# Attention and a mixture of experts on one core: rows of an intermediate at a pitch of 2112 bytes, V loaded for two pairs, a view of the output for each write, and the order made anew

## The chip, the cores and the metric

The kernel runs on one core of a Trainium2 chip. The metric is the device time of one execution in microseconds (us), median over several runs. TensorE (PE), VectorE (DVE), ScalarE (ACT) and GpSimd (POOL) compute. SyncE (SP) issues the plain transfers of this kernel, POOL the indirect ones, which gather or scatter rows by index.

## What is computed

```python
scores = 0.125 * q @ k.T              # 4 batches, 8 heads, 768 positions, width 64
scores = where(col < 4 or 0 <= row - col < 128, scores, -1e9)
x = softmax(scores) @ v               # written as 3072 tokens x 512, heads side by side
e = argmax(x @ w_gate)                # one of 8 experts for each token
g = softmax(x @ w_gate)[e] * sigmoid((x @ w_output_gate)[e])
out[token] = g * (relu(x[token] @ w1[e]) @ w2[e])    # w1: 512 x 1024, w2: 1024 x 512
```

## The kernel before

**Attention** goes over 16 pairs of heads, four to a batch (`pair`). For a pair, SP loads q, k and V (384 KB each, V as pieces of 512 bytes), POOL scales q in place (L1097), PE makes the scores of six tiles of 128 rows (L1113), DVE masks them and takes the maximum (L1122, L1125), ACT the exponential (L1129). PE turns the result (L1149), ACT copies it to `f` (L1152), POOL makes the masked halves `g` and `f` (L311), and PE multiplies by V (L1200) into `oA` and `oB`. The first four columns go a way of their own: `pk` on POOL (L1169), a turn on PE (L1175), a copy to `hlk`, three small transfers to `psk` and a matmul (L1212). The logits of the gate are summed up by POOL in `lg` (L1246). The pair's 768 x 128 block of x is stored by SP into the DRAM tensor `xd` (L1272).

**`xd`** has one row for each token and a row of zeros ahead: 512 values of x and one value `den`, the token's weight g. In float32 a row is 2052 bytes, so that nearly all rows, and the 512-byte pieces that a pair writes into them, begin off any multiple of 64 bytes.

**Routing** of a batch (`gate_route`) is small work on DVE, POOL and PE: which expert, and which place in the expert's list. After the second and the third batch two slots each for the fullest experts are set up, four early slots of 256 tokens. After the last batch the rest is dealt to 13 slots of 64 to 384 tokens by `final_table`, some 250 small DVE instructions (L484, L690 to L777) that give indices `idx` and experts `exp_i`.

**A slot** gathers its tokens' rows from `xd` to `xg` (POOL, L802), turns them on PE (L862), splits them into a coarse part `xh` (ACT) and a rest `xl` (DVE, L867), multiplies by the expert's first weights (L981, three products for each tile), applies relu with the same split (`hh` on ACT L893, `hl` on DVE L896), multiplies by the second weights (L1019), scales by `den`, which ACT copies to `sc` (L885), and scatters `y` to the output (POOL, L878). Weights come as 512 KB pieces to `raw` and are split by ACT (L837) and DVE (L841). The names `wa`, `wb`, `wc` with `h` or `l` are buffers of split weights.

**Order.** The work is recorded first (`Plan.op`), with an assumed duration, what it reads and writes, and a wished time `at`, made of the pair's or slot's number and of offsets in the table `AT`. `Plan.order` then deals the operations to the engines in turn, among those that could start nearly at once the one with the lowest `at`. The order is fixed when the program is built. Each engine runs its instructions in that order, and a waiting instruction holds up all that stand behind it on its engine or queue. The assumed durations, among them `size` and `busy` of transfers, do nothing but set this order.

**Waits for writes.** Two writes to one tensor are ordered by a wait. All 28 scatters name the whole of `out`, so each waits until the one before has landed.

Of the kernel before, what the change touches and what calls it, by code (L numbers as in the profile page):

```python
# [7 lines left out]
F32 = mybir.dt.float32  # L8
# [19 lines left out]
XW = DM + 1  # L28
SCALE = 0.125
# [19 lines left out]
SOFT = 1810  # L49
SLOT0, STEP, PLAIN, FSTEP = 182180, 20000, 1, 800  # L50
# [4 lines left out]
    "load": -19780, "v": 10768, "vs": 163198, "sinkv": -13952, "scale0": 28418, "scale1": -104693, "scale2": 64567,  # L55
    "s0": 4872, "s1": 1285, "s2": 725, "s3": 1220, "s4": 5238, "s5": 1946, "fold": -23950, "exp": 61170, "tr0": 39353,
    "tr1": 74543, "tr2": 36830, "trc": 21273, "mask": -30694, "pack": 5280, "guard": -60086, "skT": -9303, "hl": -24231,
# [202 lines left out]
def act(n, k=1):  # L260
    return {"took": 165 + 0.83 * n, "busy": 60 + 0.83 * n}
# [21 lines left out]
def moe_kernel(tc, qT, kx, vx, vs, wgo, w1, w2, nsink, window, out):  # L283
# [7 lines left out]
    with ctx:  # L291
# [9 lines left out]
        xd = dram.tile([NTOK + 1, XW], F32, name="xd")  # L301
# [98 lines left out]
        def small_loads():  # L400
            q = nc.sync

            def load():
                q.dma_start(out=wgt, in_=wgo)
                for j, src in enumerate((nsink, window)):
                    q.dma_start(out=nsw_i[:, j, :], in_=src.bitcast(I32).partition_broadcast(P))
                q.dma_start(out=xd[0, 0:DM].rearrange("(p c) -> p c", p=P), in_=tab[:, 0, 0, 0:4])
                q.dma_start(out=xd[0:1, DM:XW], in_=tab[0:1, 0, 0, 0:1])
            pl.op("SP", 2500, load, w=["wgt", "nsw_i", "xd0"], size=64, busy=2400, at=3000)
            pl.op("DVE", 1500, scalars, r=["nsw_i"], at=30000)  # L410
# [8 lines left out]
        req, rdd, rpos = (st([P, T, E], F32, n) for n in ("eq", "dd", "pos"))  # L419
        rohb = st([P, T, E], BF16, "ohb")  # L420
# [6 lines left out]
        def gate_route(p, b, lg, at, step, counted=None):  # L427
# [72 lines left out]
            def d2():  # L500
                nc.vector.scalar_tensor_tensor(out=rden, in0=rz, scalar=1.0, in1=rden, op0=ALU.add, op1=ALU.mult)
                nc.vector.reciprocal(out=rden, in_=rden)
# [38 lines left out]
            v(dve(12, 2), d2, r=["z", "den"], w=["den"])  # L541
# [327 lines left out]

        def put(p, key, ysk, m, sck, where, rows_, ids, idk, at):  # L870
# [9 lines left out]
            p.op("ACT", fn=scale_, r=[ysk, sck], w=[yk], at=at, **act(m))  # L880
            p.op("POOL", 1200, write, r=[yk, idk], w=[("out", key)], at=at, size=512 * P * 4, busy=1200, land=1000)

# [19 lines left out]
        def slot(p, k, size, ids, idk, xds, n, at, plain=False, reg=None, part=None, behind=()):  # L902
# [17 lines left out]
            if half:  # L920
# [24 lines left out]
                put(p, (k, 0), ys, m, scs[0], out.rearrange("n (a c) -> (n a) c", a=2), 2 * NTOK, lambda: ids(2, 0), idk, at + 5000)  # L945
# [65 lines left out]
            for tiles in ((2,), (0, 1)) if nt == 3 else (range(nt),):  # L1011
# [11 lines left out]
                for s in tiles:  # L1023
                    put(p, (k, s), ys[s], DM, scs[s], out, NTOK, lambda s=s: ids(1, s), idk, at + 12000)
# [27 lines left out]
        for fam, n, pool in (("q", 3, "qk"), ("k", 3, "qk"), ("e", 2, "qk"), ("v", 2, "bp"), ("vsr", 1, "bp"), ("x", 2, "bp"),  # L1052
# [3 lines left out]
                             ("hh", 4, "m0"), ("y", 2, "m0")):  # L1056
# [10 lines left out]
        def pair(p):  # L1067
# [125 lines left out]
            def av(kt):  # L1193
                def fn():
                    v_, f_, g_ = get(v), get(f), get(g)
                    for t, src in ((kt, f_), (kt + 1, g_)):
                        for a in range(2) if t < T else ():
                            r = slice(a * D, (a + 1) * D)
                            o = get(oA)[r, t, :] if t < 4 else get(oB)[r, t - 4, :]
                            nc.tensor.matmul(out=o, lhsT=v_[:, kt, r], rhs=src[:, kt, a, :], start=t == kt == 0 or t == kt + 1 == 4,  # L1200
# [54 lines left out]
            def norm(g):  # L1255
# [8 lines left out]
                def fn():  # L1264
# [8 lines left out]
                  w=[("xd", b, hp)], at=(at, "st"), size=P * 4 * S, busy=400)  # L1273
# [210 lines left out]
        with mctx:  # L1484
# [58 lines left out]
```

## Time and profile before

| | |
|---|---|
| three runs | 583.05, 587.39 (median), 591.72 us |
| the profiled execution | 590.12 us, its span 588.2 us |
| PE, DVE, ACT, POOL busy | 519.1, 346.5, 280.7, 193.9 us |
| mean granted clock of PE | 0.955 of full speed |
| DMA | 112.60 MB, 191 GB/s over the span |

The span is the time from the first to the last instruction, 1.9 us less than the execution's own time. A busy time is the union of an engine's instructions. The clock is granted by a throttle in two levels, 1.0 (2.4 GHz) and 0.5 (1.2 GHz).

### The profile page before, as it was taken

What the parts mean: (1) busy time and instruction counts of PE and PEld (TensorE: products, weight loads), DVE (VectorE), ACT (ScalarE), POOL (GpSimd) and SP (SyncE); (2) the same over time, 40 slices, a digit from 0 to 9 for tenths busy, and PEclk for the clock granted to TensorE, in tenths of its full rate; (3) what the DMA queues carried; (4) which work ended last, traced back from release to release, by engine and by line L of the source; (5) the groups of instructions that cost most, each with busy time, mean ns of one, the idle gap of its engine ahead of it and who ended that gap; (6) DMA issues with size and microseconds to landing.
All of it is one profiled execution on the core that took longest, in us unless ns stands there. A gap on an engine that the chain in (4) does not pass through costs nothing. (4 is left out here: it accounts for less than half of the span.)

```text
span 588.2 us, 10368 instructions
## 1 busy us (share of the span) xinstructions
PE 519.1 (88%) x3480; PEld 402.6 (68%) x3480; DVE 346.5 (59%) x802; ACT 280.7 (48%) x741; POOL 193.9 (33%) x296
## 2 busy tenths in 40 slices
PE   4998799987889899995889899999999878999992
PEld 2565576654556585784769598898778766787971
DVE  5765777768668837489985235425636445465420
ACT  3665667754655645434434325525435445256320
POOL 8546676566475611035011131212210302101010
PEclk9998889978979999996999899999999989999998
DMA  7474757648996149825448954627797728967640
GB/s 222 145 121 118 142 117 191 118 114 204 323 317 102 42 145 174 290 63 184 168 129 294 344 200 149 213 108 244 263 329 267 233 76 306 336 217 264 203 163 18
DMA packets 68959, 112.60 MB, mean 191 GB/s; under 512 B 8316, under 2 KB 35200, under 8 KB 68898
## 3 DMA queue, kind: packets, MB, share of 16 engines
q1 hardware_dynamic: 64434, 97.94, 56.4%
q0 software_dynamic: 4464, 13.91, 6.7%
q8 instruction: 30, 0.49, 0.3%
q14 instruction: 31, 0.25, 0.2%
HBM read 98.26 MB, written 13.25 MB: 190 GB/s over the span
## 5 line engine op out<-in xcount | busy, mean ns | idle before, releaser
L1129 ACT ACTIVATE e<-s,nmx 128x132 f32<-128x132 f32 x192 | 69.8, 371 | 49.1 <-DVE nmx L1125 44.2
L1113 PE MATMUL s<-k,q 64*128 64x260 f32 (+1 forms) x384 | 69.6, 442 | 12.9 <-POOL q L1097 6.2
L878 POOL DMA_INDIRECT out_dram<-y,idx x20 | 22.2, 1110 | 147.1 <-ACT y L875 96.6
L896 DVE SCALAR_TENSOR_TENSOR hl<-s,hh 128x512 fp32r<-128x512 f32 (+1 forms) x36 | 26.7, 747 | 58.4 <-ACT hh L893 58.3
L1113 PEld LDWEIGHTS s<-k,q 64*128 64x128 f32 x384 | 37.4, 205 | 29.5 <-ACT e L1129 14.3
L893 ACT ACTIVATE hh<-s 128x512 fp32r<-128x512 f32 (+1 forms) x36 | 23.0, 645 | 72.3 <-PE s L981 69.2
L802 POOL DMA_INDIRECT xg<-xd,idx x21 | 23.5, 1119 | 93.4 <-PE tp L862 65.8
L1122 DVE COPY_PREDICATED s<-maskf,s 128x256 f32<-128x256 int32 x80 | 33.9, 424 | 28.0 <-PE s L1113 24.0
L1097 POOL TENSOR_SCALAR q<-q 128x256 f32<-128x256 f32 x48 | 41.5, 875 | 22.2 <-DMA q<-in_qT_dram 16.0
L1125 DVE TENSOR_REDUCE nmx<-s 128x2 f32<-128x264 f32 x96 | 41.5, 432 | 3.3
L1129 ACT ACTIVATION_READ_ACCUMULATOR e<-s,nmx 128x1 f32 x192 | 38.7, 201 | 0.0
L311 POOL TENSOR_SCALAR_AFFINE_SELECT g<-f 128x512 f32<-128x512 f32 (+1 forms) x48 | 27.1, 565 | 23.5 <-ACT f L1152 23.3
L1149 PE MATMUL tp<-ident,e 128*128 128x128 f32 x192 | 33.0, 301 | 1.8 <-DVE lw L1236 1.0
L1152 ACT COPY f<-tp 128x512 f32<-128x512 f32 x48 | 28.1, 588 | 13.1 <-PE tp L1149 12.6
L875 ACT ACTIVATE y<-oA,sc 128x512 f32<-128x512 f32 (+1 forms) x18 | 11.7, 651 | 41.0 <-PE oA L1019 34.6
L867 DVE TENSOR_TENSOR xl<-tp,xh 128x512 fp32r<-128x512 f32 x23 | 15.5, 686 | 26.2 <-ACT xh L865 26.2
L1149 PEld LDWEIGHTS tp<-ident,e 128*128 128x128 f32 x192 | 23.5, 153 | 10.0 <-issue 3.7
L311 POOL TENSOR_SCALAR_AFFINE_SELECT f<-f 128x512 f32<-128x512 f32 (+1 forms) x48 | 26.9, 561 | 3.3
L1200 PE MATMUL oA<-f,v 128*64 128x128 f32 x256 | 27.1, 291 | 0.0
L878 POOL DMA_INDIRECT out_dram<-y,idx_e x8 | 9.7, 1214 | 49.1 <-ACT y L875 24.5
L1265 DVE TENSOR_TENSOR x<-tp,rs 128x512 f32<-128x512 f32 (+1 forms) x32 | 17.5, 550 | 13.8 <-PE tp L1262 13.7
L862 PE MATMUL tp<-ident,xg 128*128 128x128 f32 (+1 forms) x112 | 16.0, 271 | 4.2 <-ACT hr L935 2.5
(549 smaller groups left out, 1540.2 us busy)
## 6 DMA issues: line engine op xcount, KB each, us to landing
raw<-in_w_dram SPq DMA_DIRECT2D x96, 512.0 KB
v<-in_vx_dram SPq DMA_DIRECT2D x16, 384.0 KB
xd<-x SPq DMA_DIRECT2D x16, 384.0 KB
k<-in_kx_dram SPq DMA_DIRECT2D x15, 396.0 KB
q<-in_qT_dram SPq DMA_DIRECT2D x15, 384.0 KB
wa2h<-in_w_dram SPq DMA_DIRECT2D x4, 512.0 KB
wa2l<-in_w_dram SPq DMA_DIRECT2D x4, 512.0 KB
wa1h<-in_w_dram SPq DMA_DIRECT2D x3, 512.0 KB
```

The source lines that it names most:

```text
L311: nc.gpsimd.affine_select(out=ap, in_=ap if src is None else src, pattern=pattern, compare_op=op, fill=fill, base=base, channel_multiplier=cm)
L802: nc.gpsimd.indirect_dma_start(out=p.get(key), out_offset=None, in_=xd[0:n + 1, :], in_offset=bass.IndirectOffsetOnAxis(ap=ids(), axis=0))
L878: nc.gpsimd.indirect_dma_start(out=where, out_offset=bass.IndirectOffsetOnAxis(ap=ids(), axis=0), in_=p.get(yk)[:, 0:m], in_offset=None, b ...
L896: nc.vector.scalar_tensor_tensor(out=p.get(hl)[:, :, 0:n], in0=p.get(ps)[:, :, 0:n], scalar=0.0, in1=p.get(hh)[:, :, 0:n].bitcast(F32), op ...
L1097: nc.gpsimd.tensor_scalar(out=c, in0=c, scalar1=SCALE, scalar2=None, op0=ALU.mult)
L1113: nc.tensor.matmul(out=get(s)[:, a, o0:P + CW], lhsT=get(q)[r, t * P:(t + 1) * P], rhs=get(k)[r, k0:k0 + P + CW - o0], start=True, stop=True)
L1122: nc.vector.copy_predicated(out=both[:, :, 4:CW], mask=bc(maski[:, 1, 4:CW], 1, 2), data=z[:, :, 0:P])
L1125: nc.vector.tensor_reduce(out=get(nmx)[:, t, :], in_=both, axis=AX.X, op=ALU.max, negate=True)
L1129: nc.scalar.activation(out=get(e)[:, t, a, :], in_=get(s)[:, a, P:P + CW], func=AF.Exp, bias=get(nmx)[:, t, a:a + 1], scale=1.0, accum_out ...
L1149: nc.tensor.transpose(out=get(tp)[:, i, :], in_=get(e)[:, 2 * j + i // 2, i % 2, 4:CW], identity=ident)
L1152: nc.scalar.copy(out=get(f)[:, two].rearrange("p t a r -> p (t a) r"), in_=get(tp))
L1200: nc.tensor.matmul(out=o, lhsT=v_[:, kt, r], rhs=src[:, kt, a, :], start=t == kt == 0 or t == kt + 1 == 4, stop=False, skip_group_check=True)
```

## The change

- A row of `xd` has 528 values (`XP`), 2112 bytes, a multiple of 64. `den` is written 16 times into the row's end, so the small store goes from 4 to 64 bytes for each token, and the reciprocal before it from 6 to 96 columns. A gather brings 2112 bytes for each token.
- V is loaded for two pairs by one transfer of 768 KB, in pieces of 1024 bytes, 8 transfers in place of 16, into tiles of twice the size.
- Each scatter names a view of `out` of its own, declared disjoint from the others, and does not wait for the one before.
- All four buffers of `y` lie in the pool that opens when attention is done; before, two were there from the start.
- In the planner, a store of x counts as 786 KB in place of 393 KB, V as 904 KB, the store of `den` as 400 KB in place of 3 bytes. ACT's assumed durations are changed a little. The table `AT`, `SOFT` and `SLOT0` have new numbers, and the order comes out new on all engines.

```diff
+XP = 528
-SOFT = 1810
-SLOT0, STEP, PLAIN, FSTEP = 182180, 20000, 1, 800
+SOFT = 7200
+SLOT0, STEP, PLAIN, FSTEP = 153718, 20000, 1, 800
...
-    "n0": -84793, "n1": 56715, "xm": -63859, "st": -71391, "rt": 46575, "ft": 3923, "near": 77,
+    "add": -71892, "n0": -64048, "n1": 74649, "xm": -90144, "st": -74470, "rt": 75760, "ft": 46913, "near": 73,
...
-        xd = dram.tile([NTOK + 1, XW], F32, name="xd")
+        xd = dram.tile([NTOK + 1, XP], F32, name="xd")
...
-                nc.vector.reciprocal(out=rden, in_=rden)
+                nc.vector.reciprocal(out=rdenw, in_=bc(rden, 2, XP - DM))
...
-                nc.sync.dma_start(out=rows(b)[:, :, DM:XW], in_=rden.unsqueeze(2))
-            p.op("SP", 2500, store, r=["den"], w=[("xd", b, "den")], at=next(clock), size=3, busy=400)
+                nc.sync.dma_start(out=rows(b)[:, :, DM:XP], in_=rdenw)
+            p.op("SP", 2500, store, r=["den"], w=[("xd", b, "den")], at=next(clock), size=400000, busy=400)
...
-            new(p, "xg", [P, XW], key=key)
+            new(p, "xg", [P, XP], key=key)
...
+        views = iter(dram_disjoint_views(out, NT_MAX * (NE + NSLOT)))
+        def where(k):
+            return out if k == "rest" else next(views)
...
-                    put(p, (k, s), ys[s], DM, scs[s], out, NTOK, lambda s=s: ids(1, s), idk, at + 12000)
+                    put(p, (k, s), ys[s], DM, scs[s], where(k), NTOK, lambda s=s: ids(1, s), idk, at + 12000)
...
-            v = new(pl, "v", [P, T, P], key=("v", p))
-            pl.op("SP", 2000, lambda: nc.sync.dma_start(out=get(v), in_=vx[b, :, :, hp * P:(hp + 1) * P].rearrange("t p c -> p t c")),
-                  w=[v], at=(at, "v"), size=P * 4 * S, busy=400)
+            v = ("v", p // 2)
+            if p % 2 == 0:
+                new(pl, "v", [P, T, 2 * P], key=v)
+                pl.op("SP", 2000, lambda: nc.sync.dma_start(out=get(v), in_=vx[b, :, :, hp * P:(hp + 2) * P].rearrange("t p c -> p t c")),
+                      w=[v], at=(at, "v"), size=P * 8 * S * 1.15, busy=400)
...
-                  w=[("xd", b, hp)], at=(at, "st"), size=P * 4 * S, busy=400)
+                  w=[("xd", b, hp)], at=(at, "st"), size=P * 8 * S, busy=400)
```

What the new order does is shown at three places. The first is SP's queue about 33 us into the run. There `xd<-x` is the store of a pair's block, `v<-`, `q<-` and `k<-` are loads for later pairs, `psk<-hlk` the three small transfers. Before:

```order
L1272 DMA xd<-x_475 128x6x128
L1079 DMA v_580<-in_vx_dram 128x6x128
L1076 DMA q_596<-in_qT_dram 128x768
L1076 DMA k_606<-in_kx_dram 128x792
L1188 DMA psk_204<-hlk_665 8x5x128 x3
L1079 DMA v_719<-in_vx_dram 128x6x128
L1272 DMA xd<-x_624 128x6x128
L1076 DMA q_739<-in_qT_dram 128x768
L1076 DMA k_749<-in_kx_dram 128x792
```

and after the change:

```order
L1282 DMA xd<-x_474 128x6x128
L1089 DMA v_579<-in_vx_dram 128x6x256
L1084 DMA q_592<-in_qT_dram 128x768
L1084 DMA k_598<-in_kx_dram 128x792
L1198 DMA psk_205<-hlk_651 8x5x128 x3
L1282 DMA xd<-x_618 128x6x128
L1084 DMA q_726<-in_qT_dram 128x768
L1084 DMA k_731<-in_kx_dram 128x792
```

The sequence of store, V, q, k stays, with a V of twice the width in it, and the next pair has no V load.

The second place is DVE where early slot 2 needs its `xl` and the final table is being made (`idx`, `key`, `top`, `who`, `units`, `less`, `off`, `some`, `pos` belong to routing and table). Before:

```order
L747 SCALAR_TENSOR_TENSOR idx<-idx,upp 128x12
L713 SCALAR_TENSOR_TENSOR key<-units,less 128x8
L714 TENSOR_REDUCE top<-key 128x1
L715 TENSOR_SCALAR who<-key,top 128x8
L867 TENSOR_TENSOR xl_3384<-tp_3332,xh_3352 128x4x128
L719 SCALAR_TENSOR_TENSOR units<-who,units 128x8
L719 SCALAR_TENSOR_TENSOR less<-who,less 128x8
L719 SCALAR_TENSOR_TENSOR off<-who,off 128x8
L867 TENSOR_TENSOR xl_3384<-tp_3340,xh_3352 128x4x128
```

and after:

```order
L870 TENSOR_TENSOR xl_3292<-tp_3270,xh_3289 128x4x128
L870 TENSOR_TENSOR xl_3292<-tp_3277,xh_3289 128x4x128
L844 TENSOR_TENSOR wc2l<-raw_3234,wc2h 128x1024
L487 TENSOR_TENSOR pos<-tp_3301,base 128x48
L488 TENSOR_TENSOR base<-tp_3301,base 128x8
L693 TENSOR_TENSOR some<-base,iouj 128x128
```

Both `xl` of the slot now stand ahead of the whole of the last batch's counting (`pos`) and of the final table (`some` is its first row); before, more than a third of the table stood ahead of them.

The third place is POOL late in the run, with the waits of each row. `DMASW` is the landing of an earlier indirect transfer, `Activation` that ACT has written `y`. The `49` is part of the semaphores' names. Before:

```order
L878 DMA out_dram<-y_5111,idx 3072x512 [waits DMASW1_49,DMASW0_49,Activation_49]
L878 DMA out_dram<-y_5121,idx 3072x512 [waits DMASW1_49,Activation_49]
L802 DMA xg_5164<-xd,idx 128x513 [waits DMASW3_49,PE_49]
L802 DMA xg_5169<-xd,idx 128x513 [waits PE_49]
L878 DMA out_dram<-y_5198,idx 6144x256 [waits DMASW2_49,Activation_49]
```

and after:

```order
L805 DMA xg_5083<-xd,idx 128x528 [waits DMASW1_49,PE_49]
L883 DMA out_dram<-y_5076,idx 3072x512 [waits DMASW2_49,Activation_49]
L883 DMA out_dram<-y_5085,idx 3072x512 [waits DMASW3_49,Activation_49]
L805 DMA xg_5116<-xd,idx 128x528 [waits DMASW4_49,PE_49]
L805 DMA xg_5370<-xd,idx 128x528 [waits DMASW5_49,PE_49]
```

The first of the two gathers now stands ahead of the two scatters, and the second of these scatters waits for a semaphore that the first one does not raise. Before, it waited for `DMASW1`, the landing of the first.

## Rows read from the trace of the kernel before

**Rows 1.** The page's head: the span, and busy time of each engine with its share of the span and its instructions.

```profile
span 588.2 us, 10368 instructions
PE 519.1 (88%) x3480; PEld 402.6 (68%) x3480; DVE 346.5 (59%) x802; ACT 280.7 (48%) x741; POOL 193.9 (33%) x296
```

**Rows 2.** Busy time by stretch: attention until PE has its last score tiles, and the rest until PE ends. Columns: stretch, its length, busy time of PE, PE's weight loads, DVE, ACT, POOL with instructions, then PE's granted clock, the busy share of the DMA engines and GB/s.

```profile
0.00:206.00 206.00, 175.58 (x1531) 119.95 (x1532) 144.94 (x437) 121.79 (x505) 130.54 (x238) 0.93 0.66 163
206.00:577.30 371.30, 343.49 (x1952) 282.63 (x1950) 201.54 (x365) 158.27 (x236) 62.39 (x58) 0.97 0.64 212
```

**Rows 3.** PE's instructions in order of time, at four stalls in attention. Columns: start, length in us, engine, line, operation, tiles; in brackets the idle time before and what ended it.

```profile
46.66 0.69 PE L1200 MATMUL oB<-g,v 128*64 128x128 f32 x4 [2.50 <-POOL g L311]
...
71.58 0.20 PE L472 MATMUL tp<-ohb,upper 128*128 128x48 bf16 x1 [2.84 <-DVE ohb L449]
...
120.42 0.44 PE L1200 MATMUL oB<-g,v 128*64 128x128 f32 x4 [1.78 <-POOL g L311]
...
164.34 0.40 PE L1175 MATMUL tp<-ident,pk 128*40 128x128 f32 x1 [3.29 <-POOL pk L1169]
```

**Rows 4.** POOL's instructions in order of time, ahead of these four stalls; same columns.

```profile
44.35 0.85 POOL L1097 TENSOR_SCALAR q<-q 128x256 f32<-128x256 f32 x1 [3.44 <-DMA q<-in_qT_dram]
45.17 0.85 POOL L1246 TENSOR_TENSOR lg<-lg,lw 128x96 f32<-128x96 f32 x2
45.97 0.64 POOL L311 TENSOR_SCALAR_AFFINE_SELECT g<-f 128x512 f32<-128x512 f32 x1
...
67.20 1.67 POOL L1097 TENSOR_SCALAR q<-q 128x256 f32<-128x256 f32 x2 [2.10 <-DMA q<-in_qT_dram]
...
116.47 1.67 POOL L1097 TENSOR_SCALAR q<-q 128x256 f32<-128x256 f32 x2 [4.57 <-DMA q<-in_qT_dram]
...
160.81 1.68 POOL L1097 TENSOR_SCALAR q<-q 128x256 f32<-128x256 f32 x2 [4.01 <-PE s L1113]
```

**Rows 5.** SP's issues in order of time, ahead of the first of these stalls; same columns, the length is that of issuing.

```profile
33.51 0.41 SPq L1272 DMA_DIRECT2D xd<-x  x1
35.12 0.39 SPq L1079 DMA_DIRECT2D v<-in_vx_dram  x1
36.67 0.34 SPq L1076 DMA_DIRECT2D q<-in_qT_dram  x1
```

**Rows 6.** Busy time by stretch, columns as in rows 2: a stretch before the first store of x, with loads of V, q and k alone; a stretch just behind that store; one late in the run behind a scatter to the output.

```profile
25.00:31.00 6.00, 5.53 (x43) 3.19 (x43) 4.32 (x11) 5.54 (x24) 3.42 (x7) 1.00 0.61 205
35.50:40.50 5.00, 5.00 (x37) 2.75 (x35) 3.27 (x9) 4.34 (x18) 2.17 (x5) 1.00 1.29 81
...
499.00:507.00 8.00, 7.40 (x36) 5.29 (x36) 4.89 (x8) 4.05 (x7) 2.35 (x3) 1.00 0.84 300
```

**Rows 7.** Busy time by stretch, columns as in rows 2: six stretches in which PE was granted half the clock.

```profile
46.68:50.09 3.41, 3.40 (x22) 2.56 (x22) 0.42 (x1) 0.00 (x0) 2.27 (x3) 0.50 0.01 3
70.58:77.40 6.82, 5.82 (x41) 4.69 (x40) 5.44 (x23) 3.21 (x13) 2.60 (x4) 0.50 0.12 36
121.77:128.60 6.83, 6.83 (x34) 4.10 (x29) 4.45 (x16) 4.80 (x22) 4.77 (x8) 0.50 0.39 111
162.73:169.56 6.83, 4.92 (x31) 3.92 (x31) 2.53 (x8) 2.74 (x11) 6.20 (x10) 0.50 1.06 359
268.55:278.79 10.24, 5.85 (x27) 5.86 (x28) 9.75 (x41) 1.99 (x4) 6.19 (x5) 0.50 0.48 159
473.35:476.76 3.41, 2.85 (x13) 2.86 (x14) 1.10 (x2) 0.26 (x1) 0.00 (x0) 0.50 0.00 0
```

**Rows 8.** The first matmul of a slot (L981) alone, in a stretch at half and one at full clock. Columns: stretch, length, PE busy and matmuls, weight loads, clock, DMA share, GB/s.

```profile
274.00:278.00 4.00, 4.00 (x20) 4.00 (x20) 0.50 0.69 210
279.00:281.00 2.00, 2.00 (x20) 2.00 (x19) 1.00 0.84 269
```

**Rows 9.** PE's instructions at the start of early slot 2; columns as in rows 3.

```profile
268.06 0.38 PE L981 MATMUL s<-xh,wc3h 128*128 128x256 f32 x1 [2.54 <-ACT xh L865]
272.94 0.58 PE L981 MATMUL s<-xl,wc3h 128*128 128x256 f32 x1 [4.49 <-DVE xl L867]
...
283.84 0.39 PE L981 MATMUL s<-xh,wc3h 128*128 128x256 f32 x1 [2.46 <-DVE hl L896]
```

**Rows 10.** DVE's instructions from the count of the last batch to the indices of the first final slots and the `xl` of early slot 2; columns as in rows 3.

```profile
252.58 0.21 DVE L484 TENSOR_TENSOR pos<-tp,base 128x48 f32<-128x48 f32 x1 [1.64 <-PE tp L474]
...
270.76 0.17 DVE L747 SCALAR_TENSOR_TENSOR idx<-idx,upp 128x12 int32<-128x12 int32 x1
...
271.37 0.68 DVE L867 TENSOR_TENSOR xl<-tp,xh 128x512 fp32r<-128x512 f32 x1
...
272.20 0.68 DVE L867 TENSOR_TENSOR xl<-tp,xh 128x512 fp32r<-128x512 f32 x1
```

**Rows 11.** POOL, ACT and PE in order of time at the place of the third part of the order above; columns as in rows 3.

```profile
463.86 1.41 POOL L878 DMA_INDIRECT out_dram<-y,idx  x1 [5.98 <-ACT wa0h L837]
465.58 0.99 POOL L802 DMA_INDIRECT xg<-xd,idx  x1 [0.30 <-issue]
...
471.47 0.19 ACT L885 COPY sc<-xg 128x1 f32<-128x1 f32 x1 [6.11 <-DMA xg<-xd,idx]
...
473.91 0.58 PE L981 MATMUL s<-xh,wc0h 128*128 128x256 f32 x1 [3.59 <-DVE hl L896]
```

**Rows 12.** POOL's last instruction; columns as in rows 3.

```profile
578.25 0.97 POOL L878 DMA_INDIRECT out_dram<-y,idx  x1 [10.53 <-ACTq L1488]
```

More of the change, by code (lines that the diff above doesn't have):

```diff
@@ L5 @@
 from concourse import mybir
+from concourse.bass_types import dram_disjoint_views
 from concourse.masks import make_identity
@@ L48 @@
 PAIR, RAT = 9500, 17500
-SOFT = 1810
-SLOT0, STEP, PLAIN, FSTEP = 182180, 20000, 1, 800
+SOFT = 7200
+SLOT0, STEP, PLAIN, FSTEP = 153718, 20000, 1, 800
 AT = {
-    "load": -19780, "v": 10768, "vs": 163198, "sinkv": -13952, "scale0": 28418, "scale1": -104693, "scale2": 64567,
-    "s0": 4872, "s1": 1285, "s2": 725, "s3": 1220, "s4": 5238, "s5": 1946, "fold": -23950, "exp": 61170, "tr0": 39353,
-    "tr1": 74543, "tr2": 36830, "trc": 21273, "mask": -30694, "pack": 5280, "guard": -60086, "skT": -9303, "hl": -24231,
[3 rows of a table removed]
+    "load": -75043, "v": -26367, "vs": 183022, "sinkv": -52072, "scale0": 57340, "scale1": -114669, "scale2": 94699,
+    "s0": 9748, "s1": 9305, "s2": 9188, "s3": 8077, "s4": 5884, "s5": 10189, "fold": -52990, "exp": 22836, "tr0": 26227,
+    "tr1": 63243, "tr2": 64008, "trc": 8417, "mask": 5075, "pack": -9201, "guard": -49351, "skT": -8138, "hl": -18410,
[3 rows of a table added]
 }
@@ L260, in act @@
 def act(n, k=1):
-    return {"took": 165 + 0.83 * n, "busy": 60 + 0.83 * n}
+    return {"took": 160 + 0.865 * n, "busy": 55 + 0.87 * n}
 def gps(n, x=0.9):
@@ L407, in load @@
                 q.dma_start(out=xd[0, 0:DM].rearrange("(p c) -> p c", p=P), in_=tab[:, 0, 0, 0:4])
-                q.dma_start(out=xd[0:1, DM:XW], in_=tab[0:1, 0, 0, 0:1])
-            pl.op("SP", 2500, load, w=["wgt", "nsw_i", "xd0"], size=64, busy=2400, at=3000)
+                q.dma_start(out=xd[0:1, DM:XP], in_=tab[0:1, 0, 0, 0:XP - DM])
+            pl.op("SP", 2500, load, w=["wgt", "nsw_i", "xd0"], size=64, busy=4400, at=12000)
             pl.op("DVE", 1500, scalars, r=["nsw_i"], at=30000)
@@ L419, in moe_kernel @@
         req, rdd, rpos = (st([P, T, E], F32, n) for n in ("eq", "dd", "pos"))
+        rdenw = st([P, T, XP - DM], F32, "denw")
         rohb = st([P, T, E], BF16, "ohb")
@@ L540, in gate_route @@
             v(dve(54, 2), d1, r=["dd"], w=["den"])
-            v(dve(12, 2), d2, r=["z", "den"], w=["den"])
+            v(dve(102, 2), d2, r=["z", "den"], w=["den"])
             def store():
-                nc.sync.dma_start(out=rows(b)[:, :, DM:XW], in_=rden.unsqueeze(2))
-            p.op("SP", 2500, store, r=["den"], w=[("xd", b, "den")], at=next(clock), size=3, busy=400)
+                nc.sync.dma_start(out=rows(b)[:, :, DM:XP], in_=rdenw)
+            p.op("SP", 2500, store, r=["den"], w=[("xd", b, "den")], at=next(clock), size=400000, busy=400)
             return v
@@ L879, in write @@
                                              in_=p.get(yk)[:, 0:m], in_offset=None, bounds_check=rows_ - 1, oob_is_err=False)
-            p.op("ACT", fn=scale_, r=[ysk, sck], w=[yk], at=at, **act(m))
+            p.op("ACT", fn=scale_, r=[ysk, sck], w=[yk], at=at, took=175 + m, busy=60 + m)
             p.op("POOL", 1200, write, r=[yk, idk], w=[("out", key)], at=at, size=512 * P * 4, busy=1200, land=1000)
+        def where(k):
+            return out if k == "rest" else next(views)
         def scale_of(p, xg, key, at):
@@ L944, in slot @@
                 p.op("PE", fn=m2, r=[hf] + [w[0] for w in w2r], w=[ys], at=at + 4000, **pe(8 * f32(256), "col"))
-                put(p, (k, 0), ys, m, scs[0], out.rearrange("n (a c) -> (n a) c", a=2), 2 * NTOK, lambda: ids(2, 0), idk, at + 5000)
+                put(p, (k, 0), ys, m, scs[0], where(k).rearrange("n (a c) -> (n a) c", a=2), 2 * NTOK, lambda: ids(2, 0), idk, at + 5000)
                 return
@@ L1055, in moe_kernel @@
                              ("w", 0, "a"), ("raw", RAW, "stg"), ("xg", 4, "mx"), ("xh", 1, "mx"), ("sc", 8, "mx"),
-                             ("hh", 4, "m0"), ("y", 2, "m0")):
+                             ("hh", 4, "m0")):
             family(fam, n, pool)
@@ L1199, in fn @@
                             o = get(oA)[r, t, :] if t < 4 else get(oB)[r, t - 4, :]
-                            nc.tensor.matmul(out=o, lhsT=v_[:, kt, r], rhs=src[:, kt, a, :], start=t == kt == 0 or t == kt + 1 == 4,
+                            nc.tensor.matmul(out=o, lhsT=v_[:, kt, p % 2 * P + a * D:p % 2 * P + (a + 1) * D], rhs=src[:, kt, a, :], start=t == kt == 0 or t == kt + 1 == 4,
                                              stop=False, skip_group_check=True)
@@ L1321, in moe_kernel @@
         for fam, n, pool, gate, n0 in (("hl", 4, "mp", xq, 0), ("xl", 1, "mp", xq, 0), ("hr", 3, "mc", xa, 0), ("xf", 1, "mc", xa, 0),
-                                       ("xg", 2, "mc", xa, 4), ("y", 2, "mc", xa, 2)):
+                                       ("xg", 2, "mc", xa, 4), ("y", 4, "mc", xa, 0)):
             family(fam, n, pool, gate, first=n0)
@@ L1490, in moe_kernel @@
                 now.inst = pl.inst
-                for fam, pool in (("sc", "mx"), ("y", "m0"), ("hr", "mc"), ("xf", "mc")):
+                for fam, pool in (("sc", "mx"), ("y", "mc"), ("hr", "mc"), ("xf", "mc")):
                     family(fam, 2 if fam == "hr" else 1, pool, p=now)
```

4 rows, old and new, of the table AT are left out of this document.

## The prediction, written before the run

> **What bounds the kernel now.** I read the page's head first, then the stretches, then PE's idle times, then what the waited-for engines themselves waited for. In the head PE is busy 519.1 of 588.2 us, the next engine, DVE, 346.5 [rows 1]. So a gain must come from PE's idle time or from its clock. By stretch, PE lacks 206.00 - 175.58 = 30.4 us in attention and 371.30 - 343.49 = 27.8 us after it, at clocks of 0.93 and 0.97 [rows 2]. Whatever follows PE's end, from the last scatter at 578.25 on, about 10 us, is not touched: that scatter's wait is for ACT's branch, not for a transfer [rows 12].
>
> Half clock counts double. Twenty matmuls of one kind took 4.00 us at 0.50 and 2.00 us at 1.00 [rows 8], so half of PE's busy time in a half-clock stretch is lost. That adds to a stall what lies behind it.
>
> Three groups of stalls lie where the diff touches the order.
>
> Attention: four stalls of 2.50, 2.84, 1.78 and 3.29 us, ended by POOL's `g` and `pk` or by DVE [rows 3]; together 10.41. Ahead of each POOL had stood 3.44, 2.10, 4.57 and 4.01 us before a scaling of q; three of these waits end with q's load [rows 4]. (The fourth names PE's `s`; I put it with the others because the instruction is the same. The second stall ends with DVE's `ohb`, of routing; I count it because POOL was late just before it.) Behind each stall comes half clock, with PE busy 3.40, 5.82, 6.83 and 4.92 us [rows 7], 20.97 in all, half of it lost: 10.5. **T1 = 10.4 + 10.5 = 20.9 us.**
>
> Early slot 2: PE waits 2.54 us for `xh`, 4.49 for `xl`, 2.46 for `hl` [rows 9], together 9.49. DVE makes the table from 252.58 to 270.76, and `xl` only at 271.37 and 272.20 [rows 10]. Half clock with 5.85 us busy [rows 7] loses 2.9. **T2 = 12.4 us.**
>
> Late slots: a scatter waits 5.98 us on POOL, a gather behind it issues at 465.58, ACT's `sc` waits 6.11 for that gather, PE waits 3.59 [rows 11]. The releaser named for the scatter is a weight split by ACT; the order shows that it waits for the landing of the scatter before. Half clock with 2.85 busy [rows 7] loses 1.4. **T3 = 5.0 us.**
>
> **The change part by part.** *Pitch.* Before the first store of x, loads of V, q and k move 205 GB/s at a DMA share of 0.61. Just behind a store it is 81 GB/s at a share of 1.29: the engines are busy and move little. Behind a scatter of rows to the output, whose rows are 2048 bytes apart, it is 300 GB/s at 0.84 [rows 6]. A write to DRAM is thus not slow as such; what sets the store apart is 512-byte pieces at a pitch of 2052. No row shows 512-byte pieces at 2112. Its bounds are 81 GB/s (nothing gained) and 300 GB/s; I take 205, the rate of the loads alone, of which V's pieces have 512 bytes too.
>
> *V for two pairs.* It is 786 KB, 3.8 us at 205 GB/s in place of 1.9, and it stands at four places between a store and a q. The first: store issued at 33.51, V at 35.12, q at 36.67 [rows 5], and q's scaling started at 44.35 [rows 4], 10.8 us after the store's issue for 1.18 MB (109 GB/s). With store 1.9, V 3.8, q 1.9 us at 205 GB/s it would be 7.6 us and a landing delay that I put at 0 to 2 us: q at 41.1 to 43.1. POOL began to wait at 44.35 - 3.44 = 40.91, so 0.2 to 2.2 us of 3.44 remain, 1.3 in the middle. Between POOL's 3.44 and PE's 2.50 lies a cushion of 0.9, so about 0.4 us reaches PE. I charge each of the four places 0.4 us and, since a small stall may or may not be followed by half clock, 1.0 of the 2.6 (10.5 / 4) that it cost: 5.6 in all. **T1 gives 15**, bounds 8 (every place keeps 3.2) and 20.9. At pairs without a V load the sequence shrinks to store and q, 3.8 us: no wait. The double tiles hold V for two pairs; SP's V load then waits for an older pair's last matmul, and the q queued behind it on SP waits with it. No row prices that wait; I charge nothing, and T1's lower bound covers it.
>
> *xl before the table.* The waits for `xl` (4.49) and `hl` (2.46) go with the half clock (2.9); the 2.54 for `xh` is ACT's behind a gather and stays. **T2 gives 10**, bounds 6 and 12.4. Next late is the table: below, as a rival.
>
> *Own views, gather ahead of the scatters.* The gather no longer stands behind a wait for a landing. **T3 gives 4**, the 1.0 being kept for POOL's own issuing: 1.41 us for a scatter, 0.99 for a gather [rows 11]. Bounds 2 and 5.
>
> *Small additions.* The reciprocal goes from 6 to 96 columns: DVE took 0.17 us for 12 columns and 0.21 for 48 [rows 10], so about 0.1 us more, four times, in routing that PE rarely waits for. A gather brings 3% more bytes: the one above took from 465.58 + 0.99 to 471.47, 4.9 us, so 0.15 us more, hidden where the gather is issued early. The store of `den` keeps its 768 pieces a batch, of 64 bytes in place of 4; nothing waits for it but gathers of that batch. Its bounds are 0 and what one x store of as many pieces costs, a stall of T1's size (5.2 us) once or twice; I take 0, since four such stores run now without a stall of their own in these rows. The new `y` buffers open after attention, and the first scatter is later than that anyway.
>
> *The order made anew.* PE's idle time outside the three groups is 30.4 + 27.8 - 10.4 - 9.5 - 3.6 = 34.7 us, and every engine's sequence changes. No row can show where new stalls fall. Bounds: 0, and 10 (two stalls like slot 2's 4.49); I take 5. A gain beyond the three groups I count in none of the cases, as no row names one.
>
> **The sum.** 15 + 10 + 4 - 5 = 24 us. The profiled execution took 590.1 us: 566.1. The median of the runs is 2.7 lower: 563.4. I forecast **564**. The likeliest case alone reaches from -38 (549) to 8 + 6 + 2 - 10 = -6 (581).
>
> **The rivals,** all from the median.
>
> *All three groups go entirely, no new stall* (38.3 us): 549. For it: every second pair has no V load and the pitch may give the 300 GB/s of rows 6. Against it: `xh`'s wait has another cause.
>
> *The pitch does nothing.* The rows of x still begin at many different offsets from larger powers of two; if the slowness of rows 6 comes from 512-byte pieces being written at all, or from starts off a larger boundary than 64 bytes, the store stays as it is and T1 with it: 10 + 4 - 5 = 9 less, 578. For it: no row shows a fast 512-byte write. Against it: V's 512-byte pieces are read within loads at 205 GB/s. The Trainium skill ("DMA: Bandwidth & Descriptors", section "How a descriptor splits into AXI transactions") speaks for this rival: it says that a transaction must start on a 256-byte boundary and that a piece starting elsewhere needs one more; 2112 is 8 x 256 + 64, so three rows in four would still start off it, and by that rule the sum would stay near 578. The rule is told for reads, and no row here tells writes at the two pitches apart.
>
> *The doubled V behind a store that is still slow* (the other side). At 81 GB/s a double V takes 9.7 us in place of 4.9, so q comes 4.9 us later at each of four places: 19.4 us. With 9 gained elsewhere the kernel is 10 slower, 598; if each place also brings a half-clock stretch of its own (2.6), 608; I take 603. It decides from 9 / 4 = 2.3 us for each place on. For it: q is what POOL waits for [rows 4]. Against it: the pitch must fail first, and the pairs without V catch up.
>
> *The table's stall moves to early slot 4.* The table took 18.2 us [rows 10] and now starts behind both `xl`; DVE is 201.54 / 371.30 = 54% busy after attention [rows 2], so with all that work ahead of it it could take 18.2 / 0.46 = 40 us, and the gather 4.9 more. PE has two slots for that time, by an even share of 371.30 us over 17 slots 44 us. If it is late T2 moves instead of going: 15 + 4 - 5 = 14 less, 573.
>
> **How the numbers follow.** Chances: forecast 0.47, everything gone 0.17, pitch without effect 0.16, slow double V 0.09, table's stall moved 0.11. From 547 to 582 lie nearly all of the first, two thirds of the second, most of the third and all of the last: 0.8. A change of 2% is about what runs that spread from 583.05 to 591.72 can tell from none; the limits are 575.6 and 599.1. Faster: 0.45 + 0.17 + 0.03 + 0.08 = 0.73; slower 0.06; same 0.21.
>
> **What the profile after would show.** Pitch: just behind a store near 200 GB/s with a share well under 1.29, and POOL's waits for q below 1 us where there is no V. T1: PE's clock in attention above 0.93 and its idle time there near 18 us. T2: no PE wait for `xl` in early slot 2; a wait for slot 4's gather would show the moved stall. T3: no scatter waiting on POOL for a landing. I am wrong if the rate behind a store stays near 80 GB/s, or if PE's idle time comes back at places that none of these parts touch.

## The result, and the profile after

| | before | changed |
|---|---|---|
| median of the runs beside each other | 586.99 us | 547.96 us (547.02 to 550.96) |
| ratio, with its 95% interval | | 0.9344 (0.9277 to 0.9411) |
| the profiled execution, and its span | 590.12, 588.2 us | 550.96, 549.0 us |

The change makes the kernel 6.6% faster, 39 us by the medians. The forecast was 564, 23 us faster.

The head of the page after the change, as [rows 1]:

```profile
span 549.0 us, 10360 instructions
PE 505.8 (92%) x3480; PEld 394.7 (72%) x3480; DVE 349.1 (64%) x802; ACT 280.1 (51%) x741; POOL 193.4 (35%) x296
```

PE has the same 3480 matmuls and is busy 13 us less. Most of that is time no longer spent at half the clock: before, 39.5 us of PE's busy time lay in half-clock stretches, now 16.3, and half of the difference is 11.6. To compare kernels whose parts lie at different times I cut each run in three by its work. The first part ends with PE's last score tile (attention). The third is the last 225 us of PE's work counted at full clock. The second, between them, holds the last routing, the final table and the early slots. Here are the windows of the changed kernel (columns as in rows 2):

```profile
0.00:176.70 176.70, 158.73 (x1457) 107.04 (x1457) 140.20 (x416) 117.56 (x494) 124.15 (x229) 0.99 0.57 188
176.70:308.40 131.70, 119.71 (x733) 98.66 (x732) 95.54 (x263) 56.83 (x94) 34.70 (x36) 0.97 0.59 196
308.40:540.30 231.90, 227.35 (x1295) 188.98 (x1293) 113.39 (x123) 105.02 (x153) 33.58 (x31) 0.99 0.66 232
```

and of the kernel before, cut in the same way:

```profile
0.00:199.60 199.60, 170.57 (x1480) 115.62 (x1482) 141.05 (x422) 118.92 (x494) 126.98 (x233) 0.93 0.68 166
199.60:338.10 138.50, 122.03 (x716) 97.74 (x718) 92.81 (x259) 58.62 (x97) 28.88 (x29) 0.94 0.62 192
338.10:577.30 239.20, 226.47 (x1288) 189.23 (x1284) 112.62 (x122) 102.53 (x151) 37.07 (x34) 0.99 0.64 220
```

What PE loses in a part is its idle time (length less busy) and half of its busy time in half-clock stretches. The changed kernel has four of these before PE ends, before it had nine:

```profile
156.07:159.48 3.41, 3.34 (x22) 2.35 (x24) 3.24 (x12) 1.12 (x7) 3.20 (x6) 0.50 1.07 381
275.54:278.95 3.41, 3.41 (x19) 3.41 (x18) 3.27 (x17) 0.00 (x0) 0.00 (x0) 0.50 0.70 261
302.84:309.67 6.83, 6.12 (x19) 5.32 (x20) 1.97 (x6) 0.70 (x2) 3.18 (x4) 0.50 1.02 366
497.40:500.81 3.41, 3.41 (x16) 2.02 (x18) 2.52 (x3) 1.75 (x3) 1.27 (x2) 0.50 0.77 273
```

In attention, for one, that is 176.70 - 158.73 = 18.0 idle and 3.34 / 2 = 1.7: 19.6 us. PE's end less its losses is 495.7 to 499.5 us in every kernel of this study that has a row in the table below, so a difference between two of them is one of losses. The table is the account of the study. The tail is the span's end less PE's end.

| kernel | attention | early slots | late slots | tail | time against the kernel before |
|---|---|---|---|---|---|
| before | 41.1 | 22.8 | 14.1 | 10.9 | 1 |
| before + pitch of 2112 | 24.8 | 20.6 | 15.1 | 10.9 | 0.9665 (0.9594 to 0.9736) |
| before + pitch of 2080 | 23.0 | 21.9 | 14.5 | 10.9 | 0.9618 (0.9542 to 0.9693) |
| before + pitch of 2064 | 24.1 | 23.4 | 12.4 | 10.9 | 0.9644 (0.9591 to 0.9698) |
| before + views | 44.8 | 25.1 | 7.7 | 8.7 | 0.9837 (0.9781 to 0.9892) |
| before + pitch + views | 24.4 | 22.4 | 6.9 | 8.8 | 0.9539 (0.9454 to 0.9624) |
| new order and V | 36.5 | 18.5 | 5.7 | 10.9 | 0.9659 (0.9534 to 0.9783) |
| new order and V + views | 39.8 | 18.1 | 5.7 | 8.8 | 0.9601 (0.9508 to 0.9694) |
| new order and V + pitch | 20.8 | 20.8 | 4.8 | 10.9 | 0.9403 (0.9332 to 0.9475) |
| changed | 19.6 | 16.1 | 6.9 | 8.7 | 0.9344 (0.9277 to 0.9411) |
| changed, measured again | 20.1 | 20.7 | 6.2 | 8.7 | 0.9318 (0.9268 to 0.9369) |
| changed, V in two transfers | 20.3 | 20.7 | 6.8 | 8.8 | 0.9319 (0.9240 to 0.9398) |
| changed, pitch of 2080 | 19.0 | 18.5 | 4.8 | 8.8 | 0.9280 (0.9240 to 0.9320) |

The kernel before had medians of 586.99 to 593.12 us in the four sets of runs, so kernels of different sets are compared by these ratios. Some executions fall into a slower state; the ratios use the others alone, the medians in the text all runs. "New order and V" has the later `y` buffers too. The losses come from one profiled execution each. The two rows of the same changed kernel show how far that can vary: 16.1 and 20.7 in the early slots, with 12.0 and 12.2 us idle in both and the rest half clock.

### The profile page after: what moved, and what is told of

Its sections match the earlier page's. It is cut to its first block, busy times and chain, and to the rows that moved or that the text cites. A ratio compares the mean times of both kernels' runs of the same rounds, so it can differ in the third digit from the quotient of the medians.

```text
span 549.0 us, 10360 instructions
## 1 busy us (share of the span) xinstructions
PE 505.8 (92%) x3480; PEld 394.7 (72%) x3480; DVE 349.1 (64%) x802; ACT 280.1 (51%) x741; POOL 193.4 (35%) x296
## 4 chain that ended last, share of the span: by engine, by line
PE 58%; DVE 15%; issue 11%; DMA 6%; ACT 6%; POOL 2%; SPq 0%; another core or an unknown queue 0%; POOLq 0%; ACTq 0%; DVEq 0%
PE s L989 15%; PE oA L1027 9%; PE s L1123 7%; PE oB L1027 5%; DMA raw<-in_w_dram 5%; PE oA L1210 3%; PE tp L1159 3%; PE s L970 3%; ACT e L1139 2%; PE s L1002 2%; PE tp L1272 2%; DVE nmx L1135 2%; DVE s L1132 2%; PE oB L1210 1%; PE oA L950 1%
## 5 line engine op out<-in xcount | busy, mean ns | idle before, releaser
L1123 PE MATMUL s<-k,q 64*128 64x260 f32 (+1 forms) x384 | 66.3, 425 | 15.1 <-ACT e L1139 7.0
L1123 PEld LDWEIGHTS s<-k,q 64*128 64x128 f32 x384 | 34.4, 196 | 33.7 <-ACT e L1139 18.5
L1132 DVE COPY_PREDICATED s<-maskf,s 128x256 f32<-128x256 int32 x80 | 33.9, 424 | 21.9 <-PE s L1123 13.9
L1159 PE MATMUL tp<-ident,e 128*128 128x128 f32 x192 | 31.9, 291 | 1.3 <-ACT f L1162 0.6
L313 POOL TENSOR_SCALAR_AFFINE_SELECT f<-f 128x512 f32<-128x512 f32 (+1 forms) x48 | 28.6, 597 | 3.3
L1159 PEld LDWEIGHTS tp<-ident,e 128*128 128x128 f32 x192 | 21.9, 146 | 10.6 <-issue 3.5
L1210 PEld LDWEIGHTS oA<-f,v 128*64 128x64 f32 x256 | 14.6, 139 | 8.7 <-issue 6.7
```

The source lines that it names most:

```text
L313: nc.gpsimd.affine_select(out=ap, in_=ap if src is None else src, pattern=pattern, compare_op=op, fill=fill, base=base, channel_multiplier=cm)
L1123: nc.tensor.matmul(out=get(s)[:, a, o0:P + CW], lhsT=get(q)[r, t * P:(t + 1) * P], rhs=get(k)[r, k0:k0 + P + CW - o0], start=True, stop=True)
L1132: nc.vector.copy_predicated(out=both[:, :, 4:CW], mask=bc(maski[:, 1, 4:CW], 1, 2), data=z[:, :, 0:P])
L1159: nc.tensor.transpose(out=get(tp)[:, i, :], in_=get(e)[:, 2 * j + i // 2, i % 2, 4:CW], identity=ident)
L1210: nc.tensor.matmul(out=o, lhsT=v_[:, kt, p % 2 * P + a * D:p % 2 * P + (a + 1) * D], rhs=src[:, kt, a, :], start=t == kt == 0 or t == kt + ...
```

## The experiments

In each run below parts of the change are added to the kernel before, or taken from the changed kernel, with each engine's sequence as in the kernel it starts from (V in two transfers has eight more issues on SP). The edits are shown in their main lines.

**The pitch alone, in the old order.** The edit to the kernel before:

```diff
+XP = 528
-xd = dram.tile([NTOK + 1, XW], F32, name="xd")
+xd = dram.tile([NTOK + 1, XP], F32, name="xd")
...
-nc.vector.reciprocal(out=rden, in_=rden)
+nc.vector.reciprocal(out=rdenw, in_=bc(rden, 2, XP - DM))
...
-nc.sync.dma_start(out=rows(b)[:, :, DM:XW], in_=rden.unsqueeze(2))
+nc.sync.dma_start(out=rows(b)[:, :, DM:XP], in_=rdenw)
...
-new(p, "xg", [P, XW], key=key)
+new(p, "xg", [P, XP], key=key)
```

> The kernel before with rows of x at a pitch of 2112 bytes and nothing else (the store of den 64 bytes wide and gathers of 2112 bytes come with it); the order of the work and V's loads are those of before. Theory A, the pitch feeds the gain in attention: the pieces of a store of x are no longer slow, the four stalls of PE in attention and their half clock go, 15 to 21 us faster than before, 566 to 572. Theory B, the new order does it (loads issued in another sequence): the stores stay slow or their speed does not matter, 580 or more.

It is 3.4% faster by the ratio (medians 572.08 and 593.12 us). The stretch behind the first store of x, the same as the second window of [rows 6], in this kernel:

```profile
35.50:40.50 5.00, 5.00 (x37) 2.71 (x35) 3.27 (x10) 4.37 (x18) 2.18 (x5) 1.00 0.76 208
```

208 GB/s at a DMA share of 0.76, where 81 at 1.29 stood, with the same issues at nearly the same times (the store at 33.54 in place of 33.51). (The share adds up the times of all pieces that start in the stretch, over 16 engines, so it can exceed 1.) No `den` has been stored by then, the first is at 70.60 us, so the width of that store, which changes with the pitch, is not the cause. Nor are its pieces slow later: in the trace's records of single pieces, those of 4 bytes behind the four stores of `den` before took 7 to 18 ns in the mean, those of 64 bytes in this kernel 9 to 11. What POOL waits for q, its rows in the two kernels' lists of waits (total us, times, longest), before:

```profile
POOL q L1097 <- DMA q<-in_qT_dram: 16.0, 6, 4.6
```

and with the pitch:

```profile
POOL q L1099 <- DMA q<-in_qT_dram: 8.3, 8, 2.2
```

Attention loses 24.8 us in place of 41.1, a gain of 16.3; the ratio says 19.9 us. Theory A is borne out, B falls as the whole story.

**The views alone, in the old order.** The edit to the kernel before:

```diff
+views = iter(dram_disjoint_views(out, NT_MAX * (NE + NSLOT)))
+def where(k):
+    return out if k == "rest" else next(views)
...
-put(p, (k, s), ys[s], DM, scs[s], out, NTOK, lambda s=s: ids(1, s), idk, at + 12000)
+put(p, (k, s), ys[s], DM, scs[s], where(k), NTOK, lambda s=s: ids(1, s), idk, at + 12000)
```

> The kernel before with a disjoint view of the output for each scatter and nothing else. Theory A, which priced that wait at one place: POOL's 6 us wait at 464 us, PE's stall of 3.6 us behind it and its half clock go, 3 to 5 us faster, 582 to 584. Theory B, that wait was hidden or is replaced by ACT's wait: within 1 us of before.

1.6% faster, 9.7 us by the ratio (6 to 13 by its interval, 1.1 to 2.2%): about twice what theory A gave. The late slots gain 6.4 us and the tail 2.2. The other two parts show 3.7 and 2.3 us more loss than the trace of before, which is of another set of runs. In attention no scatter has been issued yet (the first is at 243.25 us in the kernel before), so the edit does not bear on the 3.7. It does change the scatters of the early slots. That the set accounts for both parts (593.12 against 586.99 us) is likely but not shown. I had priced one place (T3). The window of the late part shows all of it, PE idle 7.7 of 232.70 us at full clock, where the row of before above has 12.7 of 239.20 and a half-clock stretch:

```profile
343.80:576.50 232.70, 224.98 (x1288) 187.88 (x1284) 112.72 (x122) 102.71 (x151) 33.54 (x31) 1.00 0.66 227
```

The tail is 8.7 or 8.8 us in all kernels with views and 10.9 in all without.

**Both, in the old order.** The two edits above together.

> The kernel before with both, the pitch and the views, in the old order and with V loaded for one pair. Theory A: the two gains add, 18 to 26 us faster, 561 to 569, and what the changed kernel has beyond that (up to 548) is the worth of order and V. Theory B: at most 8 us faster, 579 or more.

562.45 us, ratio 0.9539: 27 us, 1 above theory A's range. By the table the two gains add: 24.4 in attention as with the pitch alone, 6.9 in the late slots as with the views. From here to the changed kernel (0.932 to 0.934) some 2% are left, 12 us: the new order with V's loads.

**The new order and V alone.** The edits to the changed kernel:

```diff
-XP = 528
+XP = 513
...
 def where(k):
-    return out if k == "rest" else next(views)
+    return out
```

> The changed kernel with the pitch back at 2052 bytes and the scatters naming the whole output: new order and V for two pairs alone. Theory A: the stores are slow again, now with a doubled V behind them, and attention has stalls as before or more: 575 to 600. Theory B: most of the gain is here, 550 to 558.

573.22 us, ratio 0.9659. Of the 586.99 us of the first set that is 567, between the two theories' ranges (550 to 558, 575 to 600). The stores are slow again. Behind the first (issued at 33.93):

```profile
36.00:41.00 5.00, 4.87 (x38) 2.85 (x37) 3.31 (x9) 4.55 (x20) 2.32 (x6) 1.00 1.08 91
```

91 GB/s. Yet attention loses 36.5 us, not more than before, and the late slots lose 5.7 in place of 14.1: the new order by itself has taken the scatters' waits off PE's path. So neither theory is right alone: order and V by themselves are worth 20 us of the time before, as much as the pitch by itself, and they overlap with the views in the late slots.

**The pitch taken out of the changed kernel.**

```diff
-XP = 528
+XP = 513
```

> The changed kernel with the pitch back at 2052 bytes (and den 4 bytes wide again), everything else kept: new order, V for two pairs, views. Theory A, the pitch is worth as much in the new order as in the old one, where it gave 20 us: attention gets its stalls back, 15 to 20 us slower than the changed kernel, 563 to 568. The rival of the doubled V behind a slow store: more than in the old order, 25 to 36 us, 573 to 584. Theory B, the new order has made the transfers uncritical: under 6 us, 554 or less.

Ratio 0.9601, that is 2.6 to 2.8% of the time before above the changed kernel (15 to 17 us): the lower end of theory A. Attention loses 39.8 us, 20.2 more than in the changed kernel. The rival of the doubled V asked for 25 to 36 us, and it falls in its own conditions: behind slow stores POOL waits 17.7 us for q here, against 25.6 in the old order with views and single V's. What the doubled V costs there apart from the new order was not separated.

**The views taken out of the changed kernel,** in two sets of runs.

```diff
 def where(k):
-    return out if k == "rest" else next(views)
+    return out
```

> The changed kernel with every scatter naming the whole output again, everything else kept. Theory A, the wait for the landing of the scatter before costs in any order: 5 to 9 us slower, 553 to 557. Theory C, moving the gather ahead of the scatters has already taken that wait off the path, so the views add nothing now: within 2 us of 548.

> The changed kernel with every scatter naming the whole output, once more, beside the changed kernel on the same chip. The first such run was 0.940 of the kernel before, against 0.934 for the changed kernel on another chip, and its losses in the late slots (10.1 us of PE's time, idle and half clock) were not above those of the changed kernel (12.3). Theory A, the wait costs in any order: 5 us or more above the changed kernel. Theory C, the new order has already taken it off the path: within 3 us.

Ratios 0.9403 and 0.9330 (0.9264 to 0.9397). In the second set the changed kernel itself had 0.9318, so the views are worth 0.7 us there. The first, 0.9403 against the 0.9344 of the row "changed", gives 3.5 us. Both are below A's 5 us, and too little for these runs to tell from nothing. (The 10.1 and 12.3 us in the second expectation are losses from about 300 us on; in the table's late slots they are 4.8 and 6.9.) In the first set's trace scatters do wait on POOL for the landing of an earlier one, 32.3 us in six waits:

```profile
POOL out_dram L883 <- DMA out_dram<-y,idx: 19.8, 4, 7.2
...
POOL out_dram L883 <- DMA out_dram<-y,idx_e: 12.5, 2, 7.1
```

and the late slots still lose only 4.8 us. With the gathers ahead of the scatters nothing that PE needs stands behind those waits. What the views add in this order is the tail, 10.9 against 8.7 us, which is 0.4%. So theory C holds for PE's path, and A's 5 us are not there.

**V in two transfers.** The same tiles and order, pieces of 512 bytes:

```diff
+def v_load():
+    for i in range(2):
+        nc.sync.dma_start(out=get(v)[:, :, i * P:(i + 1) * P], in_=vx[b, :, :, (hp + i) * P:(hp + i + 1) * P].rearrange("t p c -> p t c"))
-pl.op("SP", 2000, lambda: nc.sync.dma_start(out=get(v), in_=vx[b, :, :, hp * P:(hp + 2) * P].rearrange("t p c -> p t c")),
+pl.op("SP", 2000, v_load,
```

> The changed kernel with V for two pairs loaded as two transfers of 384 KB in pieces of 512 bytes, issued back to back at the same place, same tiles and same order. Theory A, the double transfer with its longer pieces brings little by itself: within 2 us of 548. Theory D, the longer pieces and the fewer transfers are what frees attention: its stalls come back in part, 5 to 15 us slower, 553 to 563.

Ratio 0.9319 beside 0.9344 and 0.9318 of the changed kernel: the longer pieces and the single transfer are worth nothing that can be measured. What it is worth to load V for two pairs at one place, rather than at two, is part of the order here and was not separated from it.

**Which pitch it takes.** The old order with pitches of 2080 and 2064 bytes, multiples of 32 and of 16. The edits to the kernel with the pitch alone:

```diff
-XP = 528
+XP = 520
```

> The kernel before with rows of x at a pitch of 2080 bytes, a multiple of 32 and not of 64, everything else as in the run with 2112 bytes in the old order (572). If a multiple of 32 bytes is enough: no slow pieces in the stores, 569 to 575. If the start has to be a multiple of 64: every second row stays slow, 578 to 588. If what mattered was only that a piece begins off a 4-byte address: 569 to 575 as well, with a mean piece near 27 ns.

```diff
-XP = 528
+XP = 516
```

> The kernel before with rows of x at a pitch of 2064 bytes, a multiple of 16 and not of 32, everything else as in the runs with 2080 and 2112 bytes in the old order (0.962 and 0.967 of the kernel before). If a piece must begin on a multiple of 32 bytes: slow pieces in every second row, a mean above 35 ns, 0.97 to 1.00 of before. If 16 are enough, or only addresses off 8 or 4 are slow: 27 to 30 ns and 0.96 to 0.97.

Both are as fast as 2112 (0.9618 and 0.9644, against 0.9665). The five microseconds about 2 us behind the first store, which the first kernel issues at 33.40 and the second at 31.80, are fast in both. At 2080:

```profile
35.50:40.50 5.00, 5.00 (x36) 2.77 (x35) 3.37 (x9) 4.32 (x18) 2.28 (x6) 1.00 0.83 247
```

and at 2064:

```profile
33.80:38.80 5.00, 5.00 (x37) 2.77 (x35) 3.28 (x9) 4.33 (x18) 2.19 (x6) 1.00 0.83 224
```

So no row needs to begin on a multiple of 64, let alone 256.

**The changed kernel again, and with a pitch of 2080.** The second has XP = 520 in place of 528.

> The changed kernel itself once more, beside the other three of this set on one chip, as their yardstick: a ratio to the kernel before of 0.928 to 0.941.

> The changed kernel with a pitch of 2080 bytes in place of 2112 (den written 8 times in place of 16, gathers 32 bytes shorter), everything else kept. If the wider den and the longer gathers cost nothing, as the prediction took: within 2 us of the changed kernel. If they cost: 2 to 5 us faster. If the new order, unlike the old, needs rows on a multiple of 64: slower by 3 or more.

553.60 and 549.78 us side by side, ratios 0.9318 and 0.9280, whose intervals overlap. The narrower `den` and the shorter gathers cost nothing that shows and may bring 2 to 4 us; these runs don't decide it.

## Why the prediction was right in kind and short by 16 us

The measured 548 us lies at the fast end of the 547 to 582 that the prediction thought likely. Its terms erred on both sides, and most of them gave too little.

**What bounds the kernel** held. PE's losses fell from 78.0 to 42.6 us, 35.4 of the 37.0 us by which it ends earlier. The tail gave 2.2, where the prediction had said that what follows PE's end was not touched. It was right that the last scatter does not wait for a transfer: it issues 1.0 us behind PE's end in both kernels (before, [rows 12]):

```profile
541.27 0.97 POOL L883 DMA_INDIRECT out_dram<-y,idx  x1 [12.83 <-ACTq L1498]
```

The gain lies behind that, 7.8 us to the end of the span in place of 9.9.

**T1, the pitch: mechanism right, size close.** Taken as 15, measured as 16.3 in the old order (20.4 between the two kernels with views) and 20.2 in the new one. The row that was chosen, 205 GB/s for a clean store, was near: 208 with the pitch in the old order. The residual at the four places with a doubled V, 5.6 us, was not there. In the changed kernel POOL's waits for q are all but gone:

```profile
POOL q L1107 <- DMA q<-in_qT_dram: 2.3, 2, 1.2
```

and no PE stall of 1.4 us or more is left in attention after its first 10 us. The stretch behind its first store, with 768 KB of V in it:

```profile
36.00:41.00 5.00, 4.87 (x36) 2.84 (x35) 3.31 (x9) 4.55 (x20) 2.31 (x6) 1.00 0.84 261
```

261 GB/s, more than the 205 that I reckoned with. That rate was of a stretch with the DMA share at 0.61 [rows 6]: it was limited by what had been issued, and I read it as what the transfers can do.

**T2, `xl` ahead of the table: half of it came back elsewhere.** Taken as 10; the early slots lost 22.8 before and 16.1 or 20.7 after, so 2 to 7. The stalls of [rows 9] are gone and three others stand in their place, PE's first instruction after the turn of a slot's rows:

```profile
245.90 0.18 PE L475 MATMUL tp<-ohb,upper 128*128 128x48 bf16 x1 [2.15 <-DVE xl L870]
...
274.84 0.83 PE L539 MATMUL tp<-rhs,ohrow 128*128 128x256 bf16 x6 [3.64 <-DVE xl L870]
...
302.82 0.47 PE L865 MATMUL tp<-ident,xg 128*128 128x128 f32 x1 [2.35 <-DVE xl L870]
```

They are no longer due mainly to the table; only at the third, two of its rows on DVE (`start`, `rem`) hold up `xl` by another 0.7 us. At the longest, PE had turned the rows by 271.20, and ACT, which must write `xh` before DVE can write `xl`, had a weight split and two `y` ahead of it:

```profile
271.03 1.04 ACT L840 CAST wa1h<-raw 128x1024 fp32r<-128x1024 f32 x1 [0.87 <-DMA raw<-in_w_dram]
271.98 0.68 ACT L880 ACTIVATE y<-oA,sc 128x512 f32<-128x512 f32 x1
272.56 0.68 ACT L880 ACTIVATE y<-oB,sc 128x512 f32<-128x512 f32 x1
273.13 1.07 ACT L868 CAST xh<-tp 128x512 fp32r<-128x512 f32 x2
```

So the rival that the stall moves was right that it moves, and wrong on the place: not the late table, but ACT's queue at each change of slot. The first indices of the table come at 284.6, and no PE stall of 1 us or more ends with the gather behind them:

```profile
L750 DVE SCALAR_TENSOR_TENSOR idx<-idx,upp x4: 164/172/173, 284.6 to 300.6; 128x12 int32<-128x12 int32 x3, 128x3 int32<-128x3 int32 x1
```

(This row gives shortest, median and longest duration in ns, and the first and last start.) No run has the new place of `xl` alone. The early slots lose 20.6 to 25.1 us in the table's six kernels with the old order and 16.1 to 20.8 in the seven with the new one.

**T3: the mechanism right, the size too small, and two cures for one illness.** Taken as 4; the late slots gained 7.2. The views in the old order gain 6.4 there, the order without them 8.4, both together 7.2, which is no sum. The prediction followed the wait at one place only; the 6.4 us show that there were more.

**The cost of the new order was the wrong sign.** I charged 5 us of new stalls and counted no gain beyond the three groups "as no row names one". In attention the new order, with V's loads, gained another 4.8 us (24.4 to 19.6) with the stores fast, and 5.0 (44.8 to 39.8, both with views) with them slow. A row of the kernel before did name a part of it, a fifth stall of attention with half clock behind it (from 138.84 us, 3.14 us of PE's busy time), where PE waits for ACT's exponential:

```profile
138.56 2.06 PE L1113 MATMUL s<-k,q 64*128 64x260 f32 x8 [2.73 <-ACT e L1129]
```

With pitch and views in the old order such a stall is still there, with 10.24 us at half clock from 123.37 us on. In the changed kernel the longest wait for `e` behind the first 10 us is about half as long. No half clock follows it in this trace, 3.41 us in the trace of the kernel measured again:

```profile
123.83 2.10 PE L1121 MATMUL s<-k,q 64*128 64x260 f32 x8 [2.45 <-ACT e L1137]
...
112.33 0.71 PE L1123 MATMUL s<-k,q 64*128 64x260 f32 x4 [1.33 <-ACT e L1139]
```

Of the 4.8 us 2.8 are half clock and 1.9 idle time. So the prediction's three groups left out a stall that its own trace showed. New stalls did come, those of T2, and are counted there.

By the forecast's own terms, then: attention 21.5 in place of 15, early slots 6.7 in place of 10, late slots 7.2 in place of 4, tail 2.2 in place of 0, and 0 in place of the charge of 5. That is 37.6, against 24; up to the 39.2 us between the two profiled executions it is PE's work at full clock, 499.3 and 497.7 us. The largest single part of the 13.6 missing is attention (6.5), then the charge for new stalls (5).

**The rivals.** *Everything gone* came out at its time of 549, but not by its reason: T2 was not gone, and the tail and the order made up for it. *The pitch does nothing* fell with the first run. The Trainium skill ("DMA: Bandwidth & Descriptors", section "How a descriptor splits into AXI transactions") says of reads that a transaction must start on a 256-byte boundary. For the writes here no price of that shows: rows at 2064, 2080 and 2112 bytes begin mostly off such a boundary, and behind their stores 208 to 247 GB/s move. *The doubled V* fell with the run without the pitch, in which the stores were slow and POOL still waited no longer for q than in the old order.

## What to carry to other kernels

Where a transfer is late, look at the DMA share beside the GB/s just behind the transfer ahead of it: a high share with a low rate (1.29 and 81 here) meant here that the one ahead was slow, and the new order of issues alone did not cure that (91 GB/s, with 36.5 of 41.1 us of loss left in attention). In the old order a row of 12 more bytes did as much as one of 60. Two changes that cure the same wait, a wait removed and a queue reordered, don't add, so price them together. A stall freed at one place can show the next engine in the same chain, which here was ACT in front of DVE.

## What the runs showed of the hardware

Pieces of 512 bytes written to DRAM at a pitch of 2052 bytes, so that three rows in four begin off the first one's place by no multiple of 16, made the store and what came behind it move 81 GB/s; at 2064, a multiple of 16, it was 224. In the trace's own records of packets the 1536 pieces from 34 to 42 us (the first store and the V behind it) took 83 ns in the mean in the kernel before, 27 in the median and up to 1248: a fifth of them, 303, took over 100 ns and had 87 of the 128 us in all. With a pitch of 2080 the mean of such pieces was 28 ns. So a few pieces are very slow, not all a little. The loads among them are hit too: V's pieces of 1024 bytes took 86 and 92 ns in the mean over attention in the two kernels with the new order and the old pitch, and 51 in the changed one. 2052 is the only slow pitch that was tried, so which property of it matters is not shown, nor whether 8 bytes would be enough. Why the span ends 2.2 us sooner behind the last scatter with the views was not tried either.
